# Local and global attention with a ReLU-squared MLP: transposing the global results on TensorE and re-ordering the splitting work

## The chip, the cores and the metric

The kernel runs on one core of a Trainium2 chip. The metric is the device time of one execution in microseconds, less is better. A core has four compute engines that run side by side, each through its own instructions in order: TensorE (PE in the profile, its weight loads PEld) multiplies matrices into PSUM, VectorE (DVE) and ScalarE (ACT) work on SBUF and PSUM, GpSimd (POOL) on SBUF alone. DMAs are issued from SyncE's queue (SP).

## The reference

For 8 batches and 8 heads there are 512 local positions and 32 global ones, with 64 numbers per head. Cut to what matters:

```python
s_g   = scale * q_g @ k_all.T            # 32 global queries see all 544 keys
out_g = softmax(s_g) @ v_all
s_ll  = where(|i - j| <= 32, scale * q_l @ k_l.T, -1e9)
s_lg  = scale * q_l @ k_g.T              # each local query also sees the 32 global keys
out_l = softmax([s_lg, s_ll]) @ [v_g, v_l]
x     = concat([out_g, out_l])           # (8 * 544, 512) after the heads are joined
h     = relu(x @ w_in)                   # 512 -> 2048
out   = (h * h) @ w_out                  # 2048 -> 512
```

Everything is float32.

## The kernel before

**Tiling.** The 4096 local rows are cut into 16 blocks of 256 queries (half of a batch), and each block into its 8 heads. One *step* t handles one head of one block (128 steps). The global rows of all batches form a 17th block, `xg`. The MLP trails by `LAG = 9` steps: in step t it does one eighth of the hidden units, m = t - 9, for the block before (`gemm1`, `act1`, `act2`, and one step later `gemm2`). The loop over t runs to 145; from step 128 on only the MLP and the last global job are left.

**Precision.** From step 16 on a float32 operand is split into a high part (rounded by a copy on ScalarE) and a low part (the rest, a subtraction on VectorE), and a product is made of three fast matmuls: high x high, high x low, low x high. Steps below 16 (`NPLAIN`) use plain float32 and other paths. Much of VectorE's and ScalarE's work is this splitting: `split_qk` and `split_qk_rest` (tile `qk`) for the queries and keys of the next step, `split_v` (tile `v`), `parts` and `parts_rest` (tiles `ph`, `ml`, `pl`) for the turned probabilities, `x_evac` (tiles `x_h`, `x_l`), `act2` (tiles `gh`, `gl`), `w_split` (tile `ws`) for the weights.

**A step from 16 on.** TensorE does `scores(t)` (tile `s`), the first half of `gemm1`, the second half, `g_scores` (the part of the global scores that this head's keys give), the first half of `gemm2`, a global product if one is due, the second half of `gemm2`, and `av(t - 1)` (tile `xa`). VectorE takes the maxima and subtracts (`softmax1`), ScalarE exponentiates (`softmax2`), VectorE scales (`softmax3`, tiles `st` and `prob`). The probabilities of step t are then turned: GpSimd separates their 16-bit halves (`turn`, tile `planes`), a DMA transposes (`turned`), and GpSimd joins them at the start of the next step (`join`, tile `joined`); then `parts` and `parts_rest`, then `av`.

**Global jobs.** Every 8 steps the global scores of four heads (a *group*) are complete. The rest of the work on a group is cut into jobs that are put into slots of later steps, `jobs[(step, place)]`; a place is a fixed spot in the body of the loop where the due jobs are issued. With d the base step of a group: load of the values `g_load_v` (d), `g_soft` and `g_exp` (d + 1), `g_norm` (d + 2), `g_split_v` of the first pair of heads and `g_turn` (d + 3), `g_join` and `g_parts` (tiles `pth`, `ptl`) and the product `g_av` of the first pair (tile `gxo`, scaled by ScalarE into `gxs`) (d + 4), its transposition `g_x` into `xg` and `g_split_v` of the second pair (d + 5), product and transposition of the second pair (d + 6, d + 7). `g_x` is four transposes of 32x32 on VectorE. In a round of 16 steps two groups pass: with r = t mod 16, the product of the first pair falls at r = 15 and 5, that of the second at r = 1 and 7.

**What sets the order.** `pe`, `ve`, `ac`, `po` and `sp` are wrappers (line 53, hence L53 in nearly all rows) that keep each engine's instructions in the order in which the program issues them, from step 17 on. Below that a scheduler may reorder. So on each engine the work queues exactly as the body of the loop writes it, and an instruction that waits holds up everything behind it on its engine. The weights come in 32 chunks; `PLAN` says in which of the steps 0 to 22 and at which of four ticks one is unpacked or split.

PSUM has 8 banks: `pt`, `s`, `xa` and `gs` have one each, `h` and `o` two.

Of the kernel before, what the change touches and what calls it, by code (L numbers as in the profile page):

```python
# [7 lines left out]
F32 = mybir.dt.float32  # L8
# [9 lines left out]
P = 128  # L18
HALF = 256
NGR = 2 * B  # L20
NT = NGR * H
# [3 lines left out]
WIN = 224  # L25
# [34 lines left out]
def attention_moe(  # L60
# [19 lines left out]

    heads = {}

    def plain(t):
# [71 lines left out]
    def scores(t):  # L155
        hd = heads[t]
        pool, tag = (ps_h, "h") if t < 8 and t % 2 else (ps_a, "s")
        s = pool.tile([P, 2, WIN], F32, tag=tag, name=f"s{t}")
        for u in range(2):
            qs, ks = slice(KC + u * P, KC + u * P + P), slice(128 * u, 128 * u + WIN)  # L160
            if plain(t):
                pe.matmul(s[:, u, :], hd["raw"][:, qs], hd["raw"][:, ks], start=True, stop=True)
            else:
                pe.matmul(s[:, u, :], hd["hi"][:, qs], hd["hi"][:, ks], start=True, stop=False)
                pe.matmul(s[:, u, :], hd["lo"][:, u * P : u * P + P], hd["hi"][:, ks], start=False, stop=True)
        hd["s"] = s
# [121 lines left out]

    state = {}

    def g_load(t):
# [110 lines left out]
    def g_av(t, pair):  # L402
        (gvh, gvl), (pth, ptl) = state["gvs"], state["gpt"]
        xo = ps_a.tile([64, P], F32, tag="xa", name=f"gxo{t}_{pair}")
        mm = []
# [4 lines left out]
        for i, (x, y) in enumerate(mm):  # L410
            pe.matmul(xo, x, y, start=i == 0, stop=i == len(mm) - 1)
        xs = p1.tile([64, P], F32, tag="xs", name=f"gxs{t}_{pair}")
        ac.activation(out=xs, in_=xo, func=AF.Copy, scale=state["gst", t][:64, pair : pair + 1])
        state["xs"] = xs

    def g_x(t, pair):
        b, grp, xs = t // 16, (t // 4) % 2, state["xs"]
        for j in range(2):
            h = 4 * grp + 2 * pair + j
            for dd in range(2):  # L420
                r = (h % 2) * 64 + 32 * dd
                ve.transpose(
                    out=xg[r : r + 32, h // 2, 32 * b : 32 * b + 32],
                    in_=xs[32 * j : 32 * j + 32, 64 * j + 32 * dd : 64 * j + 32 * dd + 32],
                )

# [182 lines left out]
    jobs = {}  # L613
    for t in range(NSTEP + LAG + 1):
# [29 lines left out]
        if live and not early:  # L644
            split_v(t)
        if live:
            softmax2(t)
        if new:
            parts(t - 1)
        if live and not early:  # L650
            softmax3(t)
            turn(t)
        if NPLAIN <= t + 2 < NT:
            load_head(t + 2)
        for place in (4, 3):
            for job, *args in jobs.pop((t, place), ()):
                job(*args)
        if done:
            evac(m // 8 - 1, (1,))
        w_tick(t, 0)  # L660
        if live and early:
            g_scores(t)
# [6 lines left out]
        if early and t + 1 < NPLAIN:  # L669
            scores(t + 1)  # L670
        if t + 1 < NT and not early:
            split_qk(t + 1)
        if run:
# [7 lines left out]
        if t + 1 == NPLAIN:  # L681
            split_qk(t + 1)
        if new:
            parts_rest(t - 1)
        if t + 1 < NT:
            split_qk_rest(t + 1)
# [5 lines left out]
        if live and t % 4 == 3 and (t // 8) % 2 == 1:  # L692
            d = t if t % 8 == 3 else t + 2
            for at, *job in (
                (d, 2, g_load_v, 0),
# [6 lines left out]
                (d + 4, 6, g_join),  # L702
                (d + 4, 3, g_parts),
                (d + 4, 0, g_av, 0),
                (max(d + 5, 17), 3, g_x, 0),
                (d + 5, 2, g_split_v, 1),
                (max(d + 6, 17), 0, g_av, 1),
                (max(d + 7, 18), 3, g_x, 1),
            ):
# [104 lines left out]
```

## Time and profile before

| | |
|---|---|
| median of 3 runs | 1071.05 us (1070.82 to 1072.33) |
| the profiled execution's own time | 1071.19 us |
| its span, first to last instruction | 1069.1 us |
| mean granted TensorE clock | 0.994 |
| busy: PE, PEld, DVE, ACT, POOL | 96%, 84%, 81%, 67%, 36% |
| the chain that ended last, by engine | PE 43%, DVE 37%, ACT 8%, issue 5%, DMA 3%, POOL 2% |

In a row of the profile, `out<-in` are the program's tile names, with shape, count, and behind the bar busy time, the mean of one in ns and the engine's idle time ahead of them. In a timeline the first number is the start, the second the duration, in us; consecutive equal instructions are put into one row (x2). In the list of waits, the columns are total us, how often, and the longest. In the view of stretches: from:to, length, then busy us of PE, PEld, DVE, ACT and POOL with the number of instructions, the granted clock, the DMA share and GB/s.

### The profile page before, as it was taken

What the parts mean: (1) busy time and instruction counts of PE and PEld (TensorE: products, weight loads), DVE (VectorE), ACT (ScalarE), POOL (GpSimd) and SP (SyncE); (2) the same over time, 40 slices, a digit from 0 to 9 for tenths busy, and PEclk for the clock granted to TensorE, in tenths of its full rate; (3) what the DMA queues carried; (4) which work ended last, traced back from release to release, by engine and by line L of the source; (5) the groups of instructions that cost most, each with busy time, mean ns of one, the idle gap of its engine ahead of it and who ended that gap; (6) DMA issues with size and microseconds to landing.
All of it is one profiled execution on the core that took longest, in us unless ns stands there. A gap on an engine that the chain in (4) does not pass through costs nothing.

```text
span 1069.1 us, 20564 instructions
## 1 busy us (share of the span) xinstructions
PE 1029.5 (96%) x7040; PEld 902.3 (84%) x7040; DVE 867.7 (81%) x2445; ACT 721.5 (67%) x1743; POOL 385.0 (36%) x544
## 2 busy tenths in 40 slices
PE   8999989999999999999999999999999999999998
PEld 6776778988898888888888889888888888889896
DVE  5689878899989888898979999898989999893311
ACT  6889766767767766767666766776667676664432
POOL 1010344444445343444444443453445353441000
PEclk9999989999999999999999999999999999999999
DMA  9772444445444544454544444545444454341000
GB/s 367 310 258 80 104 103 115 114 116 125 116 123 101 136 103 101 115 118 123 122 115 116 116 120 109 123 104 125 125 110 105 118 135 110 103 95 54 5 21 20
DMA packets 193576, 127.69 MB, mean 119 GB/s; under 512 B 143552, under 2 KB 168640, under 8 KB 193472
## 3 DMA queue, kind: packets, MB, share of 16 engines
q1 hardware_dynamic: 193328, 126.32, 44.5%
q8 instruction: 55, 0.90, 0.4%
q14 instruction: 49, 0.40, 0.1%
q10 hardware_dynamic: 144, 0.07, 0.0%
HBM read 82.84 MB, written 8.91 MB: 86 GB/s over the span
## 4 chain that ended last, share of the span: by engine, by line
PE 43%; DVE 37%; ACT 8%; issue 5%; DMA 3%; POOL 2%; SPq 0%; DVEq 0%; POOLq 0%; ACTq 0%
PE o L53 17%; PE h L53 16%; DVE prob L53 6%; DVE st L53 5%; DVE qk L53 5%; PE xa L53 4%; ACT prob L53 3%; DVE v L53 3%; PE s L53 3%; DVE gl L53 2%; PE gxo L53 2%; DVE x_l L53 2%; DVE ph L53 2%; DVE pl L53 2%; DMA raw<-in_pk_dram 2%
## 5 line engine op out<-in xcount | busy, mean ns | idle before, releaser
L53 PE MATMUL h<-x_h,ws 128*128 128x256 f32 x2048 | 391.4, 284 | 0.0
L53 PEld LDWEIGHTS h<-x_h,ws 128*128 128x128 f32 x2048 | 329.1, 192 | 0.7
L53 PE MATMUL o<-ws,gh 128*128 128x512 f32 x1024 | 324.4, 398 | 3.2 <-ACT ot L53 3.0
L53 PE MATMUL h<-x_l,ws 128*128 128x256 f32 x1024 | 290.9, 284 | 1.1 <-DVE x_l L53 1.1
L53 POOL COPY joined<-turned 128x1024 uint16<-128x1024 uint16 x112 | 155.3, 1387 | 378.1 <-DMA turned<-planes 232.9
L53 POOL COPY planes<-prob 128x448 uint16<-128x448 uint16 x336 | 171.3, 547 | 152.1 <-DVE prob L53 152.1
L53 PEld LDWEIGHTS o<-ws,gh 128*128 128x128 f32 x1024 | 182.5, 189 | 38.2 <-ACT ot L53 7.0
L53 PE MATMUL o<-ws,gl 128*128 128x512 f32 x512 | 202.1, 395 | 0.0
L53 PEld LDWEIGHTS h<-x_l,ws 128*128 128x128 f32 x1024 | 197.0, 192 | 3.2 <-DVE x_l L53 2.6
L53 ACT ACTIVATE prob<-prob,st 128x224 f32<-128x224 f32 x224 | 106.3, 475 | 90.3 <-DVE st L53 89.5
L53 DVE TENSOR_TENSOR gl<-pt,gh 128x512 fp32r<-128x512 f32 x128 | 87.5, 684 | 73.2 <-ACT gh L53 72.0
L53 DVE TENSOR_TENSOR qk<-raw,qk 64x352 fp32r<-64x352 f32 x224 | 109.1, 487 | 8.7 <-ACT qk L53 1.6
L53 PEld LDWEIGHTS o<-ws,gl 128*128 128x128 f32 x512 | 96.3, 188 | 23.1
L53 ACT ACTIVATE pt<-h 128x512 f32<-128x512 f32 x128 | 74.2, 580 | 54.3 <-PE h L53 54.0
L53 ACT CAST x_h<-xa 64x256 fp32r<-64x256 f32 x120 | 43.7, 364 | 98.2 <-PE xa L53 97.9
L53 ACT CAST ph<-joined 128x512 fp32r<-128x512 f32 x112 | 68.9, 615 | 41.2 <-POOL joined L53 39.0
L53 PE MATMUL s<-qk 128*128 128x224 f32 x448 | 83.5, 298 | 8.2 <-DVE qk L53 5.6
L53 DVE TENSOR_SCALAR st<-st 128x2 f32<-128x2 f32 x128 | 62.5, 488 | 34.0 <-ACT prob L53 29.8
L53 ACT CAST qk<-raw 128x608 fp32r<-128x608 f32 x112 | 78.1, 697 | 8.7 <-DMA raw<-in_pk_dram 8.6
L53 DVE TENSOR_TENSOR v<-raw,v 128x192 fp32r<-128x192 f32 x112 | 80.5, 719 | 0.0
L53 DVE CUSTOM_DVE_ANT_0 prob<-s,con 128x224 f32<-128x224 f32 x224 | 77.7, 382 | 3.0 <-PE s L53 1.3
L53 ACT ACTIVATE pt<-pt 128x512 f32<-128x512 f32 x128 | 74.5, 582 | 4.0
(85 smaller groups left out, 1616.9 us busy)
## 6 DMA issues: line engine op xcount, KB each, us to landing
raw<-in_pk_dram SPq DMA_DIRECT2D x112, 400.0 KB, 3.5
wr<-in_w_dram SPq DMA_DIRECT2D x32, 512.0 KB, 8.0
gv<-in_vg_dram SPq DMA_DIRECT2D x32, 320.0 KB, 3.8
out_dram<-ot SPq DMA_DIRECT2D x32, 256.0 KB, 2.4
raw<-in_pk_dram SPq DMA_DIRECT2D x15, 432.0 KB, 8.2
qr<-in_qg_dram SPq DMA_DIRECT2D x31, 64.0 KB, 3.1
turned<-planes SPq DMA_TRANSPOSE x112, 3.1
out_dram<-ot SPq DMA_DIRECT2D x8, 64.0 KB, 1.7
```

The lines of the kernel that those rows point to most:

```text
L53: r = method(*args, **kwargs)
```

## The change

It has three parts.

1. The global results `gxs` (64 rows of 128) are turned by one TensorE transpose per pair instead of four VectorE transposes of 32x32. The result goes into the 64 free columns of the bank of the scores (`s` is now allocated 512 wide), and ScalarE copies it into `xg` with two copies of 64x32 (`g_x_copy`). The product `gxo` also moves, from the bank of `xa` to that of `s`. `g_av` is cut in two: the matmuls, and the scaling `g_xs`.
2. The global jobs get new slots. There are two new places in the step (7: ahead of `softmax2`; 9: behind `turn`), and place 4, which held no job so far, now lies right behind `softmax2`. The first product moves one step on (r = 0 and 6). `g_parts` of the group at r = 15 goes to r = 0, place 9; that of the other stays. The second pair's `g_split_v` goes from the end of the step before into the same step as its product (r = 1 and 8), at place 3. Place 3 itself moves behind `parts_rest`.
3. In the body of the step, the output copy of the second tile (`evac`) comes right behind `softmax2`; `split_qk(t + 1)` and `split_qk_rest(t + 1)` go ahead of `parts(t - 1)` and `parts_rest(t - 1)`, all of them right behind `softmax3` and `turn`, ahead of the second half of the step.

```diff
     def scores(t):
-        s = pool.tile([P, 2, WIN], F32, tag=tag, name=f"s{t}")
+        s = pool.tile([P, 512], F32, tag=tag, name=f"s{t}")
+        state["s"] = s
+        s = s[:, : 2 * WIN].rearrange("p (u n) -> p u n", u=2)
...
     def g_av(t, pair):
-        xo = ps_a.tile([64, P], F32, tag="xa", name=f"gxo{t}_{pair}")
+        xo = ps_a.tile([P, 512], F32, tag="s", name=f"gxo{t}_{pair}")[:64, :P]
...
+        state["xo"] = xo
+
+    def g_xs(t, pair):
+        xo = state["xo"]
         xs = p1.tile([64, P], F32, tag="xs", name=f"gxs{t}_{pair}")
         ac.activation(out=xs, in_=xo, func=AF.Copy, scale=state["gst", t][:64, pair : pair + 1])
         state["xs"] = xs
 
     def g_x(t, pair):
-        b, grp, xs = t // 16, (t // 4) % 2, state["xs"]
+
+        if state["s"] is None:
+            state["s"] = ps_a.tile([P, 512], F32, tag="s", name=f"xt{t}_{pair}")
+        xt = state["s"][:, 2 * WIN :]
+        pe.transpose(xt, state["xs"], ident[:64, :64])
+        state["xt"] = xt
+
+    def g_x_copy(t, pair):
+        b, grp, xt = t // 16, (t // 4) % 2, state["xt"]
         for j in range(2):
-            h = 4 * grp + 2 * pair + j
-            for dd in range(2):
-                r = (h % 2) * 64 + 32 * dd
-                ve.transpose(
-                    out=xg[r : r + 32, h // 2, 32 * b : 32 * b + 32],
-                    in_=xs[32 * j : 32 * j + 32, 64 * j + 32 * dd : 64 * j + 32 * dd + 32],
-                )
+            r = slice(64 * j, 64 * j + 64)
+            ac.copy(xg[r, 2 * grp + pair, 32 * b : 32 * b + 32], xt[r, 32 * j : 32 * j + 32])
...
         if live and not early:
             split_v(t)
+        for job, *args in jobs.pop((t, 7), ()):
+            job(*args)
         if live:
             softmax2(t)
-        if new:
-            parts(t - 1)
+        for job, *args in jobs.pop((t, 4), ()):
+            job(*args)
+        if done:
+            evac(m // 8 - 1, (1,))
         if live and not early:
             softmax3(t)
             turn(t)
         if NPLAIN <= t + 2 < NT:
             load_head(t + 2)
-        for place in (4, 3):
-            for job, *args in jobs.pop((t, place), ()):
-                job(*args)
-        if done:
-            evac(m // 8 - 1, (1,))
+        for job, *args in jobs.pop((t, 9), ()):
+            job(*args)
+        if t + 1 < NT and not early:
+            split_qk(t + 1)
+        if new:
+            parts(t - 1)
+        if not early:
+            if t + 1 < NT:
+                split_qk_rest(t + 1)
+            if new:
+                parts_rest(t - 1)
+        for job, *args in jobs.pop((t, 3), ()):
+            job(*args)
         w_tick(t, 0)
+        if t >= NT:
+            state["s"] = None
...
-        if t + 1 < NT and not early:
-            split_qk(t + 1)
         if run:
             act1(m)
...
-        if new:
-            parts_rest(t - 1)
-        if t + 1 < NT:
             split_qk_rest(t + 1)
...
             d = t if t % 8 == 3 else t + 2
+            k = d + 7 if t % 8 == 7 and t + 1 < NT else d + 6
...
-                (d + 4, 3, g_parts),
-                (d + 4, 0, g_av, 0),
-                (max(d + 5, 17), 3, g_x, 0),
-                (d + 5, 2, g_split_v, 1),
-                (max(d + 6, 17), 0, g_av, 1),
-                (max(d + 7, 18), 3, g_x, 1),
+                ((d + 5, 9, g_parts) if t % 8 == 3 else (d + 4, 3, g_parts)),
+                (d + 5, 0, g_av, 0),
+                (d + 5, 0, g_xs, 0),
+                (d + 6, 7, g_x, 0),
+                (d + 6, 4, g_x_copy, 0),
+                (k, 3, g_split_v, 1),
+                (k, 0, g_av, 1),
+                (k, 0, g_xs, 1),
+                (k + 1, 7, g_x, 1),
+                (k + 1, 4, g_x_copy, 1),
```

More of the change, by code (lines that the diff above doesn't have):

```diff
@@ L81, in attention_moe @@
     heads = {}
+    state = {"s": None}
     def plain(t):
@@ L287, in x_evac @@
         heads[t] = None
-    state = {}
     def g_load(t):
```

## The prediction

> **What bounds the kernel now.** First the page's line of busy time, then stretches of one step each.
>
> ```profile
> PE 1029.5 (96%) x7040; PEld 902.3 (84%) x7040; DVE 867.7 (81%) x2445; ACT 721.5 (67%) x1743; POOL 385.0 (36%) x544
> ```
>
> TensorE is the bound, and an average of 96% hides where the rest goes. From step 17 on, every step begins with the scores matmuls, so I took the view of stretches with the starts of the scores of steps 80 to 95 as borders: one whole round of 16 steps, in which two groups of global jobs fall. Columns: stretch, length, then busy time of PE, PEld, DVE, ACT, POOL, then clock.
>
> ```profile
> 594.83:601.78 6.95, 6.95 (x54) 6.34 (x52) 6.32 (x24) 4.96 (x12) 2.56 (x4) 1.00 0.40 101
> 601.78:609.98 8.20, 8.00 (x66) 7.18 (x65) 7.14 (x20) 5.16 (x13) 3.12 (x4) 1.00 0.47 124
> ...
> 616.99:624.33 7.34, 7.25 (x53) 6.49 (x51) 6.43 (x22) 5.21 (x13) 2.75 (x4) 1.00 0.36 88
> 624.33:631.96 7.63, 7.35 (x54) 6.39 (x52) 7.42 (x19) 5.34 (x13) 4.71 (x8) 1.00 0.50 124
> 631.96:641.37 9.41, 8.48 (x63) 7.24 (x64) 9.12 (x21) 5.81 (x14) 4.75 (x5) 1.00 0.50 123
> 641.37:648.52 7.15, 7.12 (x53) 6.37 (x51) 6.39 (x21) 4.58 (x12) 2.53 (x4) 1.00 0.31 77
> 648.52:656.67 8.15, 8.06 (x63) 7.26 (x64) 7.26 (x21) 5.94 (x15) 3.14 (x4) 1.00 0.48 122
> 656.67:663.62 6.95, 6.95 (x53) 6.34 (x52) 6.19 (x21) 4.64 (x11) 2.56 (x4) 1.00 0.50 120
> ...
> 670.69:677.86 7.17, 7.17 (x53) 6.27 (x52) 5.96 (x17) 5.50 (x13) 3.25 (x4) 1.00 0.58 166
> ...
> 684.81:692.36 7.55, 7.34 (x53) 6.42 (x51) 6.73 (x22) 5.51 (x14) 2.68 (x4) 1.00 0.43 106
> 692.36:699.71 7.35, 7.26 (x51) 6.50 (x51) 7.03 (x23) 5.32 (x15) 2.76 (x4) 1.00 0.42 106
> 699.71:707.51 7.80, 7.52 (x54) 6.46 (x52) 7.51 (x18) 5.35 (x13) 4.72 (x8) 1.00 0.47 117
> 707.51:716.89 9.38, 8.48 (x64) 7.24 (x64) 9.06 (x21) 6.14 (x16) 4.73 (x5) 1.00 0.52 116
> sum 122.06, PE 118.97 PEld 105.68 DVE 111.23 ACT 85.53 POOL 53.09; mean PE 7.44 PEld 6.61 DVE 6.95 ACT 5.35 POOL 3.32
> ```
>
> A step that waits for nothing takes 6.95 us (steps 80 and 88). Steps 81, 85, 87 and 95 also hold a global product gxo. The matmuls of such a product have 128 columns, as the two of the row 663.50 below, which need 0.12 us up to the next start: 13 x 0.06 = 0.8 us. So a round is 16 x 6.95 + 4 x 0.8 = 114.4 us of work and 122.06 - 114.4 = 7.7 us of lost time. By step: 0.45 in 81, 0.4 in 83, 0.7 in 84, 1.65 in 85, 0.2 in 86, 0.4 in 87, 0.6 in 92, 0.4 in 93, 0.85 in 94, 1.65 in 95, the rest in crumbs. VectorE, at 111 of 122 us, is nearly full too. The waits of TensorE name it:
>
> ```profile
> PEld s L53 <- DVE qk L53: 16.7, 51, 2.0
> PEld gxo L53 <- DVE ptl L53: 11.3, 13, 0.9
> PEld o L53 <- ACT ot L53: 7.0, 9, 1.9
> ```
>
> The scores of the next step wait for the low halves of q and k, which VectorE makes last, behind the step's global job; gxo waits for the low half ptl of its probabilities.
>
> **The change, part by part.**
>
> Rows of two steps without a wait, 70 (start 519.54) and 88 (start 656.67):
>
> ```profile
> 522.38 0.58 DVE L53 TENSOR_SCALAR prob<-prob,st 128x224 f32<-128x224 f32 x2
> 522.88 0.84 DVE L53 STREAM_TRANSPOSE xg<-gxs 32x32 f32<-32x32 f32 x4
> 523.75 0.56 DVE L53 TENSOR_TENSOR ph<-joined,ph 32x256 fp32r<-32x256 f32 x1
> 524.99 0.98 DVE L53 TENSOR_TENSOR qk<-raw,qk 64x352 fp32r<-64x352 f32 x2
> 525.89 0.69 DVE L53 TENSOR_TENSOR gvl<-gv,gvh 128x512 fp32r<-128x512 f32 x1
> ...
> 519.54 0.65 PE L53 MATMUL s<-qk 128*128 128x224 f32 x4
> ...
> 656.67 0.65 PE L53 MATMUL s<-qk 128*128 128x224 f32 x4
> 660.17 0.63 PE L53 MATMUL o<-ws,gh 128*128 128x512 f32 x2
> 661.58 0.63 PE L53 MATMUL o<-ws,gh 128*128 128x512 f32 x2
> 663.50 0.28 PE L53 MATMUL xa<-pl,v 128*64 128x128 f32 x2
> 663.62 0.56 PE L53 MATMUL s<-qk 128*128 128x224 f32 x2
> ```
>
> *Turning.* Four times a round VectorE loses 0.84 us. ScalarE gets two copies of 64x32 each time and TensorE a transpose. Nearest rows:
>
> ```profile
> L53 ACT COPY sg<-gs 64x96 f32<-64x96 f32 x32 | 7.5, 235 | 0.0
> L53 PE MATMUL pt<-con,pr 128*128 128x128 f32 x32 | 6.5, 277 | 0.0
> ```
>
> The copies: at most 2 x 0.235 = 0.5 us on an engine busy 86 of 122 us, covered. The transpose: 6.5 / 32 = 0.2 us busy for 128 columns, half as many here: 0.1 us on TensorE, bounds 0.06 and 0.28. It shares the bank of the scores, so it stands behind softmax1. Its place is after half of gemm1, some 1.9 us into the step (gemm1 and the scores end at 660.17 - 656.67 = 3.5), and in a step without backlog softmax1, which ends a chain of two exponentials ahead of 522.38 (2.8 us in), is done by then. 4 x 0.1 = 0.4 us a round.
>
> *q and k first.* The two subtractions qk now follow the scaling of prob, ahead of the turned probabilities (ph, ml, pl) and of all global jobs but ptl of every other group. They are done some 4.5 us into the step, over 2 us before the next scores. What is late next is pl for the step's last product, two matmuls earlier than the scores. With 0.98 us of qk and 1.2 us of ph to pl (523.75 to 524.99) behind a prob that is ready 3.4 us into the step, pl comes at 5.6 us and is wanted at 6.8 (663.50 - 656.67). The global jobs now run behind all that, beside the last matmuls and the head of the next step. In 83, 84, 92, 93 and 94 the wait goes: 2.95 us a round. The 0.45 of 81 goes too.
>
> *85 and 95.* Here no reordering helps all the way.
>
> ```profile
> 631.38 0.98 DVE L53 TENSOR_TENSOR qk<-raw,qk 64x352 fp32r<-64x352 f32 x2
> 635.09 1.62 DVE L53 TENSOR_SCALAR st<-st 128x2 f32<-128x2 f32 x1
> 637.48 1.03 DVE L53 TENSOR_TENSOR ptl<-sg,pth 128x512 fp32r<-128x512 f32 x1
> 638.55 0.32 DVE L53 TENSOR_TENSOR pth<-sg,pth 64x128 fp32r<-64x128 f32 x1
> ...
> 633.65 1.37 POOL L53 COPY joined<-turned 128x1024 uint16<-128x1024 uint16 x1 [3.23 <-DMA turned<-planes]
> 634.93 1.76 POOL L53 COPY sg<-gq 128x1280 uint16<-128x1280 uint16 x1
> ```
>
> A subtraction-free instruction on two columns, st, takes 1.62 us and ends at 636.71; GpSimd's copy sg ends at 636.69. The turned global probabilities are still joined in these steps, and the time of that join hangs on a DMA whose source is made in step 84, so it stays at 12.4 us after the start of 84 while 84 shrinks to 6.95. VectorE comes to step 85 with the deferred gvl behind it (about 1.0 us late), so st again falls into the copy. From its end: prob 0.8, qk 1.0, ph to pl 1.2: pl at 12.4 + 3.0 = 15.4, 8.5 into step 85, then 0.25. New 85: 8.75 instead of 6.95, a loss of 1.8. Same in 95.
>
> *Products moved.* Out of 85, 95, 87 into 86, 80, 88; four a round stay four. In 86 the operands are a step old: no wait, and the 0.2 of 86 and 0.4 of 87 go. In 80 ptl (1.03) and pth (0.32) go first behind prob. I put prob at 4.6 us, the 3.4 of a free step plus an estimate of 1.2 for what 95 leaves over (its adds into sg and its gl, now behind a pl at 8.5). ptl, ready at 5.65, is wanted at 5.0 (gxo begins at 661.58 - 656.67 = 4.9, and its third matmul reads ptl). Loss 0.65, bounds 0 and 1.5.
>
> *The values' split.* g_split_v of the second half moves from a place in the step before into the same step as its gxo, behind qk and ph to pl. ScalarE's gvh moves with it. gvl is now queued on VectorE behind five subtractions, and behind gxo, wanted at 4.9 us, stand the second half of gemm2, the step's last product and the next scores; ScalarE (gxs, then gh) and VectorE (gl) wait with them. In the rows of step 70 (start 519.54) gvl begins at 6.35 behind the same queue with four transposes in it; without them 5.5 to 5.65, end 6.25 to 6.35. Loss 1.35, twice a round, 81 and 88; bounds 1.0 and 2.5 (VectorE 1.2 us behind).
>
> *Output copies.* The second tile of ot goes ahead of ph and qk on ScalarE. Step 90 loses its 0.2; of the 7.0 us in the waits I take 3 for the other rounds, bounds 0 and 7.
>
> *The round:* 80 +0.65, 81 -0.45 + 1.35, 83/84/92/93/94 -2.95, 85 and 95 +0.15 each, 86 -0.2, 87 -0.4, 88 +1.35, 90 -0.2, transposes +0.4: -0.15. The crumbs take it to about -0.3. Steps 24 to 127 are 6.5 rounds: -2 us.
>
> *Steps 17 to 23*, in which the weights are still split:
>
> ```profile
> 130.80:142.52 11.72, 7.94 (x51) 6.60 (x51) 8.77 (x23) 6.47 (x17) 5.23 (x8) 0.96 0.55 121
> 142.52:153.13 10.61, 10.61 (x64) 9.81 (x64) 7.80 (x21) 6.96 (x16) 4.59 (x5) 0.72 0.42 119
> ...
> ACT qk L53 <- DMA raw<-in_pk_dram: 8.6, 7, 3.5
> ```
>
> ScalarE's copy qk waits for its load. So far ph goes ahead of it and VectorE works on ph to pl meanwhile; after the change those stand behind it. Upper bound 7 x 1.2 = +8.4, lower bound -2 x 0.84 for the transposes of 17 and 18. I take +1.
>
> Sum: -2 - 3 + 1 = -4. It is made against the profiled execution, 1071.19 us (span 1069.1 plus 2.09 around it), 0.14 over the median of the runs: 1067 us.
>
> **Rivals.** *Faster: st gets ahead of GpSimd's copy.* 635.09 and 634.93 lie 0.16 us apart. If VectorE reaches the head of 85 and 95 a little earlier, or joined lands later, st runs before the copy, the losses of 1.8 there and 0.65 in 80 fall away: 4.25 x 6.5 = 28 us, 1040. For it: the margin is small. Against: the new order brings VectorE into 85 and 95 later than before, not earlier. The Trainium skill ("SBUF — State Buffer", section "Who interferes with whom") has a rule on this: the pair of ports that VectorE and GpSimd share is locked by whichever issues first, for its whole instruction. By that rule the two cases are all there is, nothing between, and the rows of st and sg agree.
>
> *Slower: the product waits for gvl longer than worked out.* The place is steps 81 and 88, where TensorE's whole tail is queued behind gxo. It decides from a VectorE 1.2 us behind at the subtraction ph (a late landing of turned, a backlog from 80): 2.5 instead of 1.35, so 2 x 1.15 x 6.5 = +15, 1082. If the idle time also slows the clock, as in step 21, which lost 0.28 x 10.61 = 3.0 us after 11.72 - 7.94 = 3.8 us of idle in step 20, or 0.8 per us, each stall of 2.5 costs 2.0 more: 2 x 2.0 x 6.5 = 26, 1108. For it: 111 us of VectorE work in 122. Against: the round frees 3.4 us of it. On the clock the Trainium skill ("TensorE: Matmul & The Clock Gate", section "HAM oscillation — how this bites in real kernels") puts the limit at idle gaps of about 3.4 us; by it no stall of this size would cost clock and this rival ends at 1082. Step 20 agrees; no run here shows where the limit lies.
>
> **How the numbers follow.** Forecast 0.55, its own range 1059 to 1076 (the bounds of start, ot and gvl, not all at one end); faster rival 0.25; slower 0.20. What can be told from no change is 0.2%, 2.1 us: below 1068.9 or above 1073.2. Of the forecast's 0.55 some 0.32 lie below, 0.13 between, 0.10 above. Faster 0.57, same 0.13, slower 0.30. The range has to reach into both rivals: 1041 to 1085.
>
> **What would show it.** Steps 83, 84, 92, 93, 94 at 7.0 us and no row of s waiting for qk; 85 and 95 near 8.75 with st still at 1.6; steps 81 and 88 near 9.1, with TensorE waiting for gvl 13 times some 1.35 us, a wait that is not in the profile before; VectorE's busy time 25 us lower. Wrong it is if gxo doesn't wait for gvl, if st is short in 85 and 95, or if the clock row shows more halved slices than before.

## The result, and the profile after

The changed kernel takes 1125.25 us, median of 4 runs (1120.23 to 1130.06), against 1070.93 us: a ratio of 1.0508 (95% interval 1.0456 to 1.056). Predicted were 1067 us, in a range of 1041 to 1085. The profiled execution took 1130.06 us with a span of 1128.3 us and a mean granted clock of 0.978 (0.994 before).

The line of busy time of the changed kernel's page:

```profile
PE 1055.9 (94%) x7072; PEld 920.1 (82%) x7072; DVE 852.0 (76%) x2317; ACT 735.1 (65%) x1807; POOL 404.5 (36%) x544
```

VectorE did get work taken off it, 867.7 to 852.0 us, and the kernel is slower all the same: the question is not how busy it is but when. The view of stretches with the steps 80 to 95 of the changed kernel (stretch, length, busy PE, PEld, DVE, ACT, POOL, clock), the same round as in the prediction:

```profile
628.74:636.85 8.11, 8.11 (x65) 7.22 (x65) 7.38 (x22) 5.29 (x13) 3.70 (x4) 1.00 0.41 100
636.85:649.18 12.33, 10.12 (x66) 8.50 (x66) 7.13 (x20) 6.35 (x16) 4.31 (x5) 0.86 0.51 131
...
656.52:663.46 6.94, 6.94 (x53) 6.36 (x52) 5.41 (x20) 5.85 (x15) 3.05 (x4) 1.00 0.24 67
663.46:671.31 7.85, 7.47 (x54) 6.45 (x52) 7.64 (x19) 5.17 (x12) 4.69 (x8) 1.00 0.54 129
671.31:680.02 8.71, 7.44 (x53) 6.45 (x52) 8.43 (x19) 4.78 (x11) 4.74 (x5) 1.00 0.45 117
680.02:687.78 7.76, 7.76 (x65) 7.12 (x65) 6.84 (x20) 5.48 (x14) 3.04 (x4) 1.00 0.38 90
...
695.11:707.15 12.04, 9.76 (x66) 8.30 (x65) 7.86 (x20) 5.41 (x13) 4.38 (x5) 0.86 0.68 140
...
743.35:751.54 8.19, 7.46 (x52) 6.45 (x52) 7.97 (x21) 5.16 (x12) 4.69 (x8) 1.00 0.60 123
751.54:761.11 9.57, 7.46 (x53) 6.46 (x52) 8.73 (x19) 5.45 (x14) 4.65 (x5) 1.00 0.43 107
sum 132.37, PE 123.11 PEld 108.49 DVE 107.92 ACT 87.20 POOL 55.48; mean PE 7.69 PEld 6.78 DVE 6.75 ACT 5.45 POOL 3.47
```

The round takes 132.37 us instead of 122.06. Two steps hold most of it: 81 and 88, with the second products, at 12.33 and 12.04 us with a clock of 0.86. From step 24 on, steps with r = 1 take 10.5 us on average and those with r = 8 11.0 (8.2 and 7.0 before). The round shown is one of the worse ones for them: without a stretch at half clock they take 9.4 to 10.4 us (seven of thirteen), with one 11.4 to 12.4. From the start of step 24 to that of step 127 it is 836.5 us instead of 783.8, and steps 17 to 23 take 70.6 instead of 63.0.

The waits of the changed kernel (total us, times, longest):

```profile
ACT qk L53 <- DMA raw<-in_pk_dram: 61.4, 68, 3.3
...
PE xa L53 <- DVE ph L53: 25.6, 33, 2.1
...
PE gxo L53 <- DVE gvl L53: 20.9, 14, 1.8
...
PE gxo L53 <- ACT gvh L53: 5.2, 6, 1.5
```

The wait of the scores for q and k is gone, as forecast. In its place TensorE waits for ph and for the values gvl and gvh, and ScalarE's copy of q and k waits for the load raw: 61.4 us, 8.6 before. Step 88, in the timeline of the changed kernel (start, duration; in brackets the idle time ahead and what ended it):

```profile
700.85 0.28 PE L53 MATMUL gxo<-gvh,pth 128*64 128x128 f32 x1 [0.68 <-ACT gvh L53]
702.73 0.27 PE L53 MATMUL gxo<-gvl,pth 128*64 128x128 f32 x1 [1.60 <-DVE gvl L53]
...
698.96 0.70 ACT L53 CAST qk<-raw 128x608 fp32r<-128x608 f32 x1 [1.44 <-DMA raw<-in_pk_dram]
...
697.95 1.68 DVE L53 TENSOR_SCALAR prob<-prob,st 128x224 f32<-128x224 f32 x2
699.69 1.22 DVE L53 TENSOR_TENSOR qk<-raw,qk 64x352 fp32r<-64x352 f32 x2
...
702.00 0.68 DVE L53 TENSOR_TENSOR gvl<-gv,gvh 128x512 fp32r<-128x512 f32 x1
...
698.13 1.37 POOL L53 COPY joined<-turned 128x1024 uint16<-128x1024 uint16 x1 [4.65 <-DMA turned<-planes]
```

The step starts at 695.11. Two things are late in it at once. On ScalarE the copy qk can begin only 3.85 us into the step, when raw has landed, and ends at 4.55. On VectorE the scaling prob takes 1.68 us instead of 0.58 and ends at 4.53; GpSimd's copy joined, late by its DMA, runs beside it. So q and k are subtracted by 5.8, not 4.5; gvl, queued behind them and ph to pl, is done at 7.6 and not at 6.3. TensorE stands idle for 0.68 + 1.60 = 2.28 us, and the clock drops to half for the next stretch. In step 81 (start 636.85) the trace puts it down to the load alone: prob is done at 3.5 there, and VectorE waits for the copy:

```profile
641.65 1.29 DVE L53 TENSOR_TENSOR qk<-raw,qk 64x352 fp32r<-64x352 f32 x2 [1.25 <-ACT qk L53]
```

In most of the other steps with r = 1 or 8 neither is late: in steps 40 and 72 q and k are done at 4.7, and TensorE is idle for 1.43 us.

### The profile page after: what moved, and what is told of

Its sections match the earlier page's. It is cut to its first block, busy times and chain, and to the rows that moved or that the text cites. A ratio compares the mean times of both kernels' runs of the same rounds, so it can differ in the third digit from the quotient of the medians.

```text
span 1128.3 us, 20593 instructions
## 1 busy us (share of the span) xinstructions
PE 1055.9 (94%) x7072; PEld 920.1 (82%) x7072; DVE 852.0 (76%) x2317; ACT 735.1 (65%) x1807; POOL 404.5 (36%) x544
## 4 chain that ended last, share of the span: by engine, by line
DVE 35%; PE 33%; ACT 13%; DMA 11%; issue 7%; POOL 0%; DVEq 0%; POOLq 0%; ACTq 0%; SPq 0%
PE o L53 13%; PE h L53 11%; DMA raw<-in_pk_dram 11%; DVE qk L53 7%; DVE prob L53 5%; DVE st L53 4%; ACT prob L53 4%; DVE ph L53 4%; PE xa L53 3%; ACT qk L53 2%; DVE pl L53 2%; DVE ml L53 2%; DVE v L53 2%; PE s L53 2%; PE gxo L53 2%
## 5 line engine op out<-in xcount | busy, mean ns | idle before, releaser
L53 PE MATMUL h<-x_h,ws 128*128 128x256 f32 x2048 | 404.1, 288 | 0.0
L53 PEld LDWEIGHTS h<-x_h,ws 128*128 128x128 f32 x2048 | 335.3, 194 | 2.8
L53 POOL COPY joined<-turned 128x1024 uint16<-128x1024 uint16 x112 | 156.0, 1393 | 384.8 <-DMA turned<-planes 247.4
L53 POOL COPY planes<-prob 128x448 uint16<-128x448 uint16 x336 | 189.3, 601 | 186.0 <-DVE prob L53 186.0
L53 PEld LDWEIGHTS o<-ws,gh 128*128 128x128 f32 x1024 | 185.4, 191 | 32.6
L53 DVE TENSOR_TENSOR qk<-raw,qk 64x352 fp32r<-64x352 f32 x224 | 137.2, 613 | 32.7 <-ACT qk L53 27.8
L53 ACT CAST qk<-raw 128x608 fp32r<-128x608 f32 x112 | 78.3, 699 | 62.0 <-DMA raw<-in_pk_dram 61.4
L53 PE MATMUL xa<-ph,v 128*64 128x128 f32 (+1 forms) x672 | 82.3, 250 | 32.8 <-DVE ph L53 25.6
L53 PEld LDWEIGHTS xa<-ph,v 128*64 128x64 f32 x672 | 61.4, 139 | 57.1 <-DVE ph L53 31.0
L53 DVE TENSOR_TENSOR x_l<-xa,x_h 64x256 fp32r<-64x256 f32 x120 | 49.7, 414 | 52.3 <-ACT x_h L53 51.8
L53 DVE TENSOR_SCALAR st<-st 128x2 f32<-128x2 f32 x128 | 57.5, 449 | 39.6 <-ACT prob L53 35.6
L53 DVE TENSOR_SCALAR prob<-prob,st 128x224 f32<-128x224 f32 x224 | 76.0, 381 | 3.9
```

Of the source, the lines that this page charges most:

```text
L53: r = method(*args, **kwargs)
```

## The experiments

All ratios are to the kernel before, measured on the same chip, with a 95% interval. "All three" are the three edits above that row; "the same" is the kernel of the row above.

| kernel | us | ratio |
|---|---|---|
| the change | 1125.25 | 1.0508 (1.0456 to 1.056) |
| change, values split a step earlier | 1094.86 | 1.0224 (1.0198 to 1.025) |
| change, turned probabilities ahead of q, k | 1124.41 | 1.0509 (1.0479 to 1.0539) |
| change, load ahead of the transposing DMA | 1141.30 | 1.0666 (1.0634 to 1.0697) |
| change, all three | 1118.83 | 1.0457 (1.0426 to 1.0488) |
| change, TensorE filled while it waits | 1121.12 | 1.0467 (1.044 to 1.0494) |
| change, values earlier, probabilities ahead | 1096.32 | 1.0241 (1.0222 to 1.026) |
| before, q and k first alone | 1080.23 | 1.0097 (1.0073 to 1.0121) |
| before, global jobs behind alone | 1121.02 | 1.0449 (1.0409 to 1.0489) |
| before, PE transposes alone | 1084.33 | 1.0121 (1.0099 to 1.0143) |
| change, global jobs ahead again | 1076.00 | 1.0039 (1.0019 to 1.006) |
| the same, probabilities ahead of q, k | 1068.89 | 0.9976 (0.9965 to 0.9987) |
| the same, VectorE transposes | 1065.29 | 0.9953 (0.9941 to 0.9966) |
| change, only the values behind | 1103.55 | 1.0303 (1.0282 to 1.0323) |

**The values a step earlier.**

```diff
-                (k, 3, g_split_v, 1),
+                (k - 1, 1, g_split_v, 1),
```

> The changed kernel with one slot altered: the split of the second pair's values stands at the end of the step before its product, not in the step of the product. Theory 1 (most of the loss is the product waiting for its values, and the halved clock after that wait): the steps with r = 1 and r = 8, 10.5 and 10.7 us on average now, fall to about 8.2, the rows of gxo waiting for gvl and gvh (20.9 and some 5 us) go, and the whole becomes 1125 - 6.5 x 4.8 = about 1094 us. Theory 2 (VectorE and ScalarE are simply late, wherever the split stands): the split delays the softmax of the next step by its 1.0 us instead, and no more than 10 us are won, 1115 or above.

1094.86 us: theory 1. Steps with r = 8 fall to 7.8 us and those with r = 1 to 8.55, no wait for gvl above 0.1 us is left, and the time at half clock falls from 47.8 to 20.5 us. 30 us of the 54 hang on the place of this one job. What is left are waits of xa for ph, 27.2 us.

**The order of the two splits.**

```diff
-        if t + 1 < NT and not early:
-            split_qk(t + 1)
         if new:
             parts(t - 1)
+        if t + 1 < NT and not early:
+            split_qk(t + 1)
         if not early:
-            if t + 1 < NT:
-                split_qk_rest(t + 1)
             if new:
                 parts_rest(t - 1)
+            if t + 1 < NT:
+                split_qk_rest(t + 1)
```

> The changed kernel with the old order inside the new place: the copies and subtractions of the turned probabilities (ph, ml, pl) ahead of those of q and k. Theory 1 (the wait for the load of raw holds up ph behind it, and ph is wanted earlier than q and k): the waits of xa for ph (25.6 us by VectorE, 7.1 by ScalarE) all but go, the scores don't wait for q and k instead in light steps, and the whole becomes about 1095 us. Theory 2 (the wait only changes its place): the scores wait for q and k again as in the kernel before (some 17 us), and the time stays above 1113.

1124.41 us: no gain. The waits of xa for ph do go (32.7 to 8.5 us, counting ScalarE's), and steps with r = 4 and 13 come down by 0.6 and 0.45, but the scores wait for q and k again (11.0 us), and gxo waits a little longer for its values (28.0 us, 26.1 in the change).

**The load ahead of the transposing DMA.**

```diff
+        if NPLAIN <= t + 2 < NT:
+            load_head(t + 2)
         if live and not early:
             softmax3(t)
             turn(t)
-        if NPLAIN <= t + 2 < NT:
-            load_head(t + 2)
```

> The changed kernel with one issue moved: the load of the next but one head stands ahead of the transposing DMA on SyncE's queue, not behind it. Theory 1 (ScalarE's 61 us of waiting for raw delay all that is queued behind it): that row falls below 10 us, the waits of TensorE for ph, gvh and gvl, 59 us with the ones at o, shrink by half or more, and the whole becomes about 1085 to 1100 us. Theory 2 (the load then competes with the transposing DMA, so joined comes later and ph with it): the row of raw goes, the idle time of GpSimd for turned grows, and less than 10 us are won.

1141.30 us, slower still: theory 2 in its mechanism, and worse than it said. The waits of that kernel:

```profile
POOL joined L53 <- DMA turned<-planes: 273.2, 70, 15.6
...
ACT qk L53 <- DMA raw<-in_pk_dram: 16.4, 6, 3.2
```

The wait for raw shrinks from 61.4 to 16.4 us, and GpSimd's wait for the turned probabilities grows from 247.4 to 273.2. Steps 17 to 23, in which the weights are still on their way, take 79.4 us instead of 70.6; from step 24 to 127 the two kernels take 836.4 and 836.5. So the loss lies in those steps: there the turned probabilities are the more urgent transfer. Behind them this run shows neither a gain nor a loss.

**All three.**

> The changed kernel with all three: values split a step earlier, turned probabilities ahead of q and k, load ahead of the transposing DMA. If the three causes are separate, the gains add: the whole falls to the kernel before or below it, 1045 to 1070 us, with the clock at 0.99 again. If they are one and the same late VectorE, it stays near the best of the three alone, above 1085 us.

1118.83 us: the gains don't add. The values' gain is there (r = 8 at 8.2 us), and the load takes it back: steps 17 to 23 take 77.6 us, and the sixth experiment, which differs from this one by the load alone, is 22.5 us faster.

**TensorE filled while it waits.** Each gxo of a second pair gets eight matmuls ahead of it, whose result is overwritten:

```diff
+        for i in range(8 if pair else 0):
+            pe.matmul(bank, wout(whi, 0, 0)[:, :P], wout(whi, 0, 0), start=True, stop=True)
```

> The changed kernel with eight extra matmuls of 512 columns (8 x 0.235 = 1.9 us of TensorE work whose result is overwritten) ahead of each second product gxo, the one that waits for its values: TensorE is busy while it would wait, and the wait for the values itself stays. Theory 1 (the idle stretch also halves the clock after it, 47.8 us at half clock now against 10.2 before, which costs up to half the difference, 19 us): half of the halved stretches go, steps with r = 8 that are now 11.4 to 12.0 come down to some 10.0, and the whole becomes about 1125 - 10 = 1115 us, though 14 x 1.9 us of work was added. Theory 2 (only the wait counts): the fill costs what the wait doesn't cover, and the time is 1125 to 1135 us.

1121.12 us, between the two theories. Steps 81 and 88 of this kernel:

```profile
630.38:640.36 9.98, 9.98 (x75) 8.82 (x74) 7.47 (x20) 6.25 (x16) 4.39 (x5) 1.00 0.53 131
...
686.21:696.36 10.15, 9.84 (x75) 8.63 (x73) 7.96 (x20) 5.61 (x14) 4.27 (x5) 1.00 0.59 132
```

With nearly 2 us of work added, these steps are shorter than before, 9.98 and 10.15 against 12.33 and 12.04, at full clock; all six of r = 1 lie between 9.98 and 10.03, where they were 9.5 to 12.3. Time at half clock falls from 47.8 to 20.5 us. So part of the loss there is the clock and not the wait: by the means of r = 1, 10.5 - 10.0 = 0.5 us a step. It comes from the two of six whose clock was halved, 11.6 and 12.3 us.

**Values earlier and probabilities ahead.** The edits of the first two together.

> The changed kernel with the values split a step earlier and ph, ml, pl ahead of q and k, the load where the change has it. Theory 1 (with the stalls at the values gone, what is left is ph behind the wait for raw): the steps with r = 4, 13 and 5 come down by 0.7, 0.6 and 0.3 us as they did in the kernel with this order alone, 1.8 x 6.5 = 12 us, steps 17 to 23 by 3, and the whole becomes about 1081 us. Theory 2 (the order changes nothing, as it did on top of the unchanged slots): 1090 to 1097 us, with the scores waiting for q and k.

1096.32 us: theory 2. With the global jobs behind, what the order wins over the values alone in some steps (r = 4: 8.0 to 7.35 us) is lost in others (r = 0: 8.2 to 9.0). Against this kernel the one with all three loses 12.1 us in steps 17 to 23 and 12.4 from step 24 to 127, so there the load ahead costs time in both.

**q and k first, alone.** The kernel before with `split_qk` ahead of `parts` and `split_qk_rest` ahead of `parts_rest`:

```diff
+        if t + 1 < NT and not early:
+            split_qk(t + 1)
         if new:
             parts(t - 1)
...
-        if new:
-            parts_rest(t - 1)
         if t + 1 < NT:
             split_qk_rest(t + 1)
+        if new:
+            parts_rest(t - 1)
```

> The kernel before with one part of the change alone: the copy and the subtractions of q and k ahead of those of the turned probabilities; slots, global transposes and the output copies stay as they were. Theory 1 (this order is the wrong way round, since the load of raw lands late and ph is wanted first): the row of ScalarE waiting for raw grows from 8.6 to some 60 us, TensorE waits for ph some 30 us in place of the 17 for q and k, and the time is about 1085 us. Theory 2 (as forecast: q and k are due first, and the waits of the scores simply go): 83, 84, 92 to 94 near 7.0 us, 1050 to 1058 us.

1080.23 us, 5 below theory 1 and 22 above theory 2. The view of stretches of this kernel: steps 83, 84, 85, then the sum of steps 17 to 23.

```profile
626.10:633.04 6.94, 6.94 (x53) 6.36 (x52) 5.87 (x21) 5.30 (x13) 2.86 (x4) 1.00 0.41 114
633.04:641.37 8.33, 7.46 (x54) 6.44 (x52) 8.05 (x20) 5.16 (x12) 4.73 (x8) 1.00 0.54 131
641.37:650.18 8.81, 8.08 (x66) 7.13 (x65) 8.40 (x20) 6.01 (x14) 4.75 (x5) 1.00 0.46 117
...
sum 70.87, PE 58.82 PEld 50.41 DVE 51.38 ACT 41.32 POOL 22.03; mean PE 8.40 PEld 7.20 DVE 7.34 ACT 5.90 POOL 3.15
```

83, 93 and the heavy 85 and 95 gain 0.4 to 0.6 us each, 84 and 94 lose 0.7 and 0.5, in which ph comes last now. From step 24 to 127 it is a draw (784.0 us against 783.8); the loss lies in steps 17 to 23, 70.87 us instead of 62.96, those in which the copy of q and k was seen to wait for its load before.

**The global jobs behind, alone.** The kernel before with place 3, without `g_parts`, moved behind `split_qk_rest`:

```diff
-        for place in (4, 3):
-            for job, *args in jobs.pop((t, place), ()):
-                job(*args)
+        for job, *args in jobs.pop((t, 4), ()):
+            job(*args)
...
+        for job, *args in jobs.pop((t, 3), ()):
+            job(*args)
...
-                (d + 4, 3, g_parts),
+                (d + 4, 4, g_parts),
```

> The kernel before with the global jobs of the last place but g_parts moved behind the subtractions of the step (ph, ml, pl, then q and k, then the job); no other part of the change. Theory 1 (the waits of the scores come from the jobs ahead of q and k, not from the order of the two splits): steps 83, 84 and 92 to 94 lose most of their 2.95 us a round and the time is about 1052 us. Theory 2 (the jobs then push the softmax of the next step back by their 0.7 to 1.0 us, and the wait returns there): 1066 to 1080 us.

1121.02 us: theory 2, and far above its 1066 to 1080. This was the same step of thought as in the prediction, and it fails by itself, without q and k first and without any job in a new step. Steps with r = 5 and 15 take 12.0 and 13.0 us (9.8 and 9.4 before): the four of twelve with no stretch at half clock 10.5 to 11.3, the other eight 12.0 to 14.9. In them the product waits for its probabilities pth, which are made from GpSimd's copy sg. In step 84 the softmax begins 2.5 us into the step, behind the norm of step 83, and not 1.0; in step 85 the copy sg ends at 5.8 us, 4.7 in the kernel before:

```profile
PE gxo L53 <- ACT pth L53: 26.2, 13, 3.5
```

**The global jobs ahead again.** The change with place 3 where it was:

```diff
-        for job, *args in jobs.pop((t, 9), ()):
-            job(*args)
+        for place in (9, 3):
+            for job, *args in jobs.pop((t, place), ()):
+                job(*args)
...
-        for job, *args in jobs.pop((t, 3), ()):
-            job(*args)
```

> The changed kernel with place 3 back where the kernel before has it, ahead of the splits of q, k and the turned probabilities; all other parts of the change stay. Theory 1 (a global job behind the subtractions of a step delays, on VectorE, the softmax of the next step, and with it planes, the transposing DMA, joined and ph; and it is this place that makes the values late for their product): the values are ready ahead of 4.9 us into the step, so steps with r = 1 and 8 come to 8.2 to 8.7 us, those with r = 4 and 14 lose some 0.5 us, and the whole becomes about 1080 us. Theory 2 (the place matters by the values alone): 1092 to 1097 us, as with the values split a step earlier.

1076.00 us: theory 1. One moved loop brings 49 of the 54 us back. Steps 81, 88 and 95 in the view of stretches of this kernel, and the sum of the round:

```profile
605.18:613.32 8.14, 8.14 (x66) 7.32 (x66) 7.68 (x20) 6.36 (x16) 3.47 (x4) 1.00 0.42 95
...
659.71:667.47 7.76, 7.76 (x66) 7.13 (x65) 6.76 (x19) 5.40 (x13) 3.49 (x4) 1.00 0.41 99
...
711.98:719.67 7.69, 7.45 (x53) 6.46 (x52) 7.23 (x17) 5.36 (x14) 4.72 (x5) 1.00 0.43 109
sum 122.60, PE 119.10 PEld 106.14 DVE 109.68 ACT 87.14 POOL 55.64; mean PE 7.44 PEld 6.63 DVE 6.86 ACT 5.45 POOL 3.48
```

The values are split in the step of their product here too, as the change has it, and 81 and 88 don't wait at all. r = 4 and 14 are not shorter (8.4 and 8.2 us), against theory 1: there xa waits for ph, behind both the job and q and k.

**Only the values behind.** The same kernel, with the second split of the values alone behind `parts_rest`.

> The changed kernel with all jobs of place 3 ahead of the splits, but the second split of the values alone left where the change puts it, behind q, k and the turned probabilities. Theory 1 (two separate causes: the values come late for their product, some 30 us, and the other jobs push back the next softmax, some 19 us): 1076 + 30 = about 1106 us, with r = 1 and r = 8 at 10.3 us and all other steps as with the jobs ahead. Theory 2 (one cause: VectorE arrives late in these steps because of the other jobs): the product waits 1.3 us as forecast, 1076 + 6.5 x 2 x 0.9 = 1088 us, or less.

1103.55 us: theory 1, two causes. The values cost 1103.55 - 1076.00 = 27.6 us, the other jobs of place 3 the remaining 1125.25 - 1103.55 = 21.7 us. Where the second sum comes from shows in steps 110 and 111, in the timelines of VectorE, SyncE's queue, GpSimd and TensorE. First the change (the steps start at 873.68 and 881.88):

```profile
873.92 0.48 DVE L53 TENSOR_TENSOR sg<-gs,sg 64x160 f32<-64x160 f32 x2
...
875.25 0.37 DVE L53 CUSTOM_DVE_ANT_0 prob<-s,con 128x224 f32<-128x224 f32 x1
...
880.76 1.23 SPq L53 DMA_TRANSPOSE turned<-planes  x1
...
883.94 1.37 POOL L53 COPY joined<-turned 128x1024 uint16<-128x1024 uint16 x1 [3.21 <-DMA turned<-planes]
...
885.39 1.62 DVE L53 TENSOR_SCALAR st<-st 128x2 f32<-128x2 f32 x1
...
889.72 0.45 PE L53 MATMUL xa<-ph,v 128*64 128x256 f32 x2 [1.15 <-DVE ph L53]
```

and the kernel with only the second values behind (854.02 and 862.35):

```profile
854.96 0.37 DVE L53 CUSTOM_DVE_ANT_0 prob<-s,con 128x224 f32<-128x224 f32 x1
...
860.24 1.23 SPq L53 DMA_TRANSPOSE turned<-planes  x1
...
863.43 1.36 POOL L53 COPY joined<-turned 128x1024 uint16<-128x1024 uint16 x1 [3.22 <-DVE x_l L53]
...
864.91 1.59 DVE L53 TENSOR_SCALAR st<-st 128x2 f32<-128x2 f32 x1
...
869.22 0.45 PE L53 MATMUL xa<-ph,v 128*64 128x256 f32 x2 [0.18 <-DVE ph L53]
```

In the change the norm of step 109 and the copies behind it still run on VectorE when step 110 begins, so the softmax begins 1.57 us into the step and not 0.94. From there it is handed on: the turning is issued at 7.08 instead of 6.22, joined begins 2.06 us into step 111 instead of 1.08, st (again held up to the end of GpSimd's copy sg) ends at 5.13 instead of 4.15, and the last product waits 1.15 us instead of 0.18. 0.6 us late on VectorE became 1.0 us at TensorE one step later. Steps with r = 15 are 9.1 us on average in the one and 7.8 in the other, steps 17 to 23 together 70.6 and 65.6.

**The turned probabilities ahead as well.** The kernel with the jobs ahead, with the edit of the second experiment.

> The same with ph, ml and pl ahead of q and k again, so that of the change there remain the PE transposes, the moved products and values, and the output copy. Theory 1 (with the jobs ahead, the order of the two splits decides some tenths in the steps with a job, and most in steps 17 to 23, where q and k first cost 8 us in the kernel before): 1065 to 1072 us. Theory 2 (the order is worth nothing): within 4 us of the kernel with jobs ahead.

1068.89 us, theory 1: 7.1 us less, and now slightly below the kernel before. So with the jobs ahead q and k first cost 7.1 us, where the prediction gave them a gain of 2.95 x 6.5 = 19.

**The PE transposes alone.** The kernel before with `g_x` and `g_x_copy` of the change and `gxo` in the bank of the scores, in the old steps (but for the first group's, one step later); within a step the transpose has its new place, around `softmax2`.

> The kernel before with the PE transposes alone: gxo in the bank of the scores, one TensorE transpose and two ScalarE copies in place of the four VectorE transposes, in the slots of before. Theory 1 (the transpose takes 0.29 us of TensorE's time, as its rows in the changed kernel show, and the 0.84 us of VectorE that it frees lie in steps where TensorE does not wait for VectorE): 6.5 x 4 x 0.29 = +7.5 us, 1076 to 1080 us. Theory 2 (VectorE at 111 of 122 us is what the waits hang on, so what it is spared comes off them): 1055 to 1068 us.

1084.33 us, 4 above theory 1. Steps 82 and 88 of this kernel, and then step 82 in the timeline of the change, the matmuls ahead of and behind a transpose:

```profile
619.60:626.94 7.34, 7.34 (x55) 6.54 (x53) 6.14 (x18) 6.64 (x17) 2.56 (x4) 1.00 0.65 173
...
666.01:673.35 7.34, 7.34 (x54) 6.54 (x53) 5.69 (x16) 4.92 (x13) 3.14 (x4) 1.00 0.39 98
```

```profile
650.99 0.28 PE L53 MATMUL h<-x_h,ws 128*128 128x256 f32 x1
651.20 0.27 PE L53 MATMUL s<-con,gxs 64*128 64x64 f32 x1
651.40 0.38 PE L53 MATMUL h<-x_h,ws 128*128 128x256 f32 x1
```

From one h to the next it is 0.41 us where it is 0.12 without a transpose: 0.29 us, the same for all 32 of the change, and the step is longer by 7.34 - 6.95 = 0.39. Four such steps a round are 4 x 0.39 x 6.5 = 10 of the 13.3 us.

**VectorE transposes again.** The kernel with jobs and probabilities ahead, with the VectorE transposes in steps with little other global work:

```diff
-                (d + 6, 7, g_x, 0),
-                (d + 6, 4, g_x_copy, 0),
+                (x[0], 3, g_x, 0),
...
+            x = (d + 8, d + 12) if t % 8 == 3 else (d + 8, d + 10)
+            if t + 1 == NT:
+                x = d + 6, d + 7
```

> The kernel with jobs and turned probabilities ahead, and the four VectorE transposes of 32x32 in place of the PE transpose and its two copies, in steps that hold no other large global job (r = 3, 7, 9, 11); the products stay in their new slots and in the bank of the scores. Theory 1 (a PE transpose lengthens each step it falls in by 0.38 us, 7.33 against 6.95, and VectorE has room for 0.84 us where no other job is due): the steps with r = 2, 7 and 9 come to 6.95 and r = 1 to 7.75, 4 x 0.38 x 6.5 = 9.9 us, and the whole becomes about 1059 us. Theory 2 (VectorE is near its limit everywhere, and what the steps win the waits of the scores take back): 1066 to 1075 us.

1065.29 us, between the theories, and the fastest of all: 0.47% below the kernel before (interval 0.34 to 0.59%). Steps 82, 85, 86, 87 and 89 of it:

```profile
605.69:612.64 6.95, 6.95 (x53) 6.34 (x52) 6.19 (x20) 6.23 (x15) 2.89 (x4) 1.00 0.81 223
...
627.28:636.29 9.01, 7.93 (x51) 6.60 (x51) 7.77 (x19) 5.23 (x13) 4.75 (x5) 1.00 0.51 129
636.29:645.94 9.65, 9.56 (x63) 8.74 (x64) 6.85 (x19) 4.90 (x13) 3.79 (x5) 0.82 0.52 123
645.94:652.88 6.94, 6.94 (x53) 6.36 (x52) 5.49 (x20) 5.25 (x13) 1.88 (x4) 1.00 0.19 38
...
660.65:667.59 6.94, 6.94 (x54) 6.36 (x52) 6.08 (x22) 5.03 (x13) 2.56 (x4) 1.00 0.61 151
```

The 0.38 us come back in the four steps, as theory 1 has it. Of the 9.9 us 3.6 are left: steps with r = 3, 4, 6 and 14 became 0.2 to 0.3 us longer on average, one of them (86 above) by a halved clock.

## Why the prediction was wrong

By the medians, with the parts taken off in the order of the last experiments, the 54.3 us are made of: the second values behind 27.6, the other jobs behind 21.7, q and k first 7.1, the PE transposes 3.6, and all the rest (products moved, output copy, other steps for the VectorE transposes; not separated) a gain of 4 to 6 us. In another order the shares differ: added alone to the kernel before, q and k first cost 9 us and the PE transposes 13. By the steps of the prediction:

- *"The global jobs now run behind all that, beside the last matmuls and the head of the next step."* This is the step that failed. Apart from 1.0 us into steps 85 and 95 and 1.2 into step 80 the delay was put at nothing, with the tail of the step as cover, and the head of the next step was named without asking what VectorE does there: the softmax, from which planes, the transposing DMA, joined, ph and the last product of the step follow. Two kernels show it from both sides: with the jobs behind and nothing else the kernel before loses 50 us, with the jobs ahead again the change wins 49. That the two sums are so near is chance, since they are made of other things: in the former the second values kept their place, and it lost most in the steps with r = 5 and 15.
- *The values' split, 1.35 us twice a round.* The mechanism was right and named in advance, the wait for gvl, 14 times; the size was off, 17.6 us for 27.6. In the thirteen steps with r = 1 and 8 TensorE is idle for 1.2 to 2.8 us, 1.8 on average. The longest stalls, as in steps 81 and 88, have the late landings that the forecast left out, of raw and of turned, and gvh is waited for as well. The other missing term is the clock, which the forecast left to a rival: at nearly the same idle time, 1.65 to 1.78 us, such a step takes 10.0 to 10.1 us at full clock and 11.4 to 11.6 with a halved stretch. And the loss hangs on the place of the job, not on its step: with place 3 ahead the split may stay in the step of its product.
- *"They are done some 4.5 us into the step", and pl at 5.6.* In steps 40 and 72 q and k are done at 4.7, near enough, but in step 88 at 5.8 and pl at 7.0. The prediction saw the wait for raw in steps 17 to 23 and did not carry it to the others. In the kernel before ph stood ahead of q and k, and ScalarE waited 8.6 us for raw in all; with the order alone it is 52.2. In the change 83 and 92 do come to 6.95, but 84, 93 and 94 take 7.8, 7.3 and 8.2, and the last product waits for ph. With the order alone the 2.95 us a round are a draw, and in steps 17 to 23 the upper bound of +8.4 is nearly what came: +7.9 with the order alone, where +1 was taken. That the wait for raw alone is the cause was not shown, since the one kernel with an earlier load lost time elsewhere.
- *85 and 95 at 8.75.* Right in eight of twelve such steps, 8.6 to 8.7 us (8.71 in step 85) with st behind the copy sg, partly by luck: 84 took 7.84 and not 6.95, and the copy ended 13.0 us after its start and not 12.4. In the other four, step 95 among them, joined landed late and st did get ahead of the copy, as the faster rival has it. These took longer, 9.5 to 10.4 us, one of them with a halved stretch. In step 95 (start 751.54), and in 69 alike, the scaling prob, which follows st, ends only with the copy, a third case that the prediction had ruled out:

```profile
754.92 0.17 DVE L53 TENSOR_SCALAR st<-st 128x2 f32<-128x2 f32 x1 [0.53 <-ACT prob L53]
755.32 3.11 DVE L53 TENSOR_SCALAR prob<-prob,st 128x224 f32<-128x224 f32 x2
...
756.57 1.72 POOL L53 COPY sg<-gq 128x1280 uint16<-128x1280 uint16 x1
```

- *80 at 8.4, 86 at 7.75, step 90 and the output copies.* Right: for r = 0 8.1 us in three of six rounds and 8.5 on average, for r = 6 7.76 in four of six, for r = 10 6.95 in six of seven.
- *The transposes, 0.1 us each.* 0.29 in the stream of matmuls and 0.38 for the step, above the upper bound of 0.28: a lone one of 64 columns between other matmuls costs more than one of 128 columns in a row of them (0.2). Why was not looked into.
- *The slower rival* ("the product waits for gvl longer than worked out") came true in place and sign, with the clock: 1108 us by its price. Its 0.8 us of clock per us of idle is near what was measured, 1.4 to 1.6 at some 1.7 us, but only six of thirteen steps paid it. It stops short of the 1125 because the jobs pushed more than that one product.
- On the clock the Trainium skill ("TensorE: Matmul & The Clock Gate", section "HAM oscillation — how this bites in real kernels") gave a limit of about 3.4 us of idle time. The measurement disagrees: from step 24 on the longest gap of TensorE in the change is 2.05 us, and its clock was halved there ten times. The kernel before showed it already: its clock was halved in step 53 behind gaps of 1.06 and 0.56 us, and step 20, which the prediction read as agreement, has no gap above 1.84.
- Of its own signs of being wrong two appeared: st was short in step 95, and the time at half clock rose from 10.2 to 47.8 us. VectorE's busy time fell by 15.7 us, not 25.

## What to carry to other kernels

Work that is put behind the urgent work of one step stands ahead of the urgent work of the next: when a queue runs in order round a loop, follow the moved instruction to what it delays there, and cost that. A tail has room only for what the head of the next iteration doesn't wait for. And when an order is reversed, look for what the old order hid, here a load that landed late and cost nothing as long as something else stood in front of its reader.

## What the runs showed of the hardware

TensorE's clock was halved, for 3.4 or 6.8 us at a time, after stretches of 3.4 us in which it was busy 0.3 to 0.7 of the time, without any long gap: two gaps of 0.68 and 1.60 us in step 88, and in the last kernel, ahead of step 86 with its clock of 0.82, gaps of together 1.1 us. In each of the fifteen traces all starts of such stretches lie whole multiples of 3.413 us apart, to within 2 ns. Cut the change from step 24 to 127 into windows on that grid: the nine in which TensorE was busy for less than half were all followed by a halving, three at 0.52 to 0.58 were not, and one at 0.64 was. Where the limit lies isn't settled here, but such a grid fits the finding that of two equal stalls one costs clock and the other none.

In the steps shown here VectorE's scaling prob, like its short instruction st, ended with GpSimd's copies where it ran beside them: prob took 3.11 us in step 95 of the change and 1.68 in step 88, 0.58 in step 70 before; st took 1.62 in step 85 before and 0.17 in step 95 of the change, ahead of the copy.

The turned probabilities are taken up by GpSimd 3.2 us after their DMA is issued in most steps, but more than 4.3 us after it in a few, in every kernel: 7 of 112 before, 12 in the change, 3 with jobs and probabilities ahead, 18 with the load moved ahead. What delays them wasn't looked into.
